# v of unit 1 loaded through GpSimd's queue instead of SP's, with a new order for all engines

## The chip, the cores and the metric

The kernel runs on one core of one Trainium2 chip. The metric is the device time of one execution in microseconds (us), taken over several runs; the median of the runs of the kernel before is 177.78 us (177.57 to 177.90, three runs). The engines are named as in the profile: PE (TensorE matmuls), PEld (its weight loads), DVE (VectorE), ACT (ScalarE), POOL (GpSimd) and SP (SyncE). SPq and POOLq are the queues through which SP and GpSimd issue transfers (DMAs).

## The reference

Two stages. The first is a linear-attention recurrence over 768 steps for each of 4 sequences and 8 heads of width 48; its output, 3072 rows of 384, goes into a feed-forward stage with a squared ReLU.

```python
for t in range(S):
    cur = einsum('bhd,bhe->bhde', u[None] * k[t], v[t])
    y[:, :, t] = einsum('bhd,bhde->bhe', r[t], state + cur)
    state = w[None, :, :, None] * state + einsum('bhd,bhe->bhde', k[t], v[t])
x = y.transpose(0, 2, 1, 3).reshape(B * S, H * D)     # 3072 x 384
out = maximum(x @ w_in, 0) ** 2 @ w_out               # w_in 384 x 2048, w_out 2048 x 384
```

## The kernel before

**Units.** The sequence is cut into 6 chunks of 128 steps; a unit is one chunk of one of the 4 sequences, so there are 24 units, numbered chunk by chunk (units 0 to 3 are the first chunk, and so on). Within a unit the recurrence is done as matrix products: r and k are scaled by powers of the decay (`wpos`, `wneg`), turned, multiplied with each other and masked; the product with v gives the inner part of y, the state of the sequence the rest.

**Steps of a unit.** `load:i:rt`, `load:i:kt`, `load:i:vt` fetch r, k and v of unit i (192 KB each, 1024 pieces of 192 bytes) into `ldr`, `ldk`, `ldv`. `scale:i:0` and `scale:i:1` (DVE, L300) scale r and k into `rkw`; `turn` (PE, L320) and `evict_rk` (ACT, L324) turn them in units 0 to 5, `turn_dma` (a transposing DMA on SP, L309) in the later ones, into `rkT`. `rk` (DVE, L329) multiplies the two; `at` (PE, L337) gives the products of r and k, `mask` (DVE, L349) masks them into `am`. `cast_v` (ACT, L304) makes the bf16 copy `vb` of v. `sums` (PE, L357 and L362) needs `rk`, `vb` and the scaled k, `y_mm` (PE, L400, from the second chunk on also L406) needs `am`, `vb` and the state. `diag_v` and `evict_y` (DVE, L371 and L415) finish y as `yb`; `state_add`, `state_decay`, `state_cast` keep the state. `x_turn` and `evict_x` (PE, ACT) turn `yb` into `xT` in units 0 to 5, `x_dma` (a transposing DMA on SP, L424) in the later ones.

**Feed-forward steps.** `mm1:i:m:s` (PE, L447) multiplies `xT` by a part of w_in: twelve products with m = 1 (units 0 to 7, one unit at a time; s is then the quarter of w_in that it reads), six wider ones with m = 2 (two units at a time, s from 0 to 7). `relu` (ACT, L455) and `square` (ACT, L462, or DVE, L464) make `g`; `mm2:i:q` (PE, L471) multiplies four blocks of `g` by quarter q of w_out; `evict_o` (ACT) and `store` (GpSimd's queue, two on SP) write the result. The last unit goes in two halves (`mm2_half`, L486).

**The order.** No scheduler runs: `SCHEDULE` is a string of some 980 words, and the program issues them one after the other, so each engine and each queue has its instructions in the order of the string. A planner wrote the string once. `name@b` names the PSUM banks that a step takes. `fill` (PE, L245) is a product without use, put where PE is to wait in the plan; there are 68, 52 of them ahead of the first `mm1`. The tile pools put waits on DMAs where a buffer is used again.

**Loads.** r, k and v of units 2 to 5 go through GpSimd's queue, all others through SP's (L278). The four quarters of w_in and the four of w_out also go through GpSimd's queue (`weights`, L288 and L291); the first quarter of w_in is released by a small GpSimd copy that reads k of unit 0, the other quarters (the held-back ones) stand further down in the order. GpSimd also computes the decay columns: `u_columns` (L264, L267) waits for the DVE copy `copy_columns` (L261), `end_columns` (L270, L272) follows later. In the kernel before the first transfers are, in order: on SP k0, r0, r1, k1, v0, v1, k6, k9, k7, r6; on GpSimd's queue r2, quarter 0 of w_in, k2, v2, r3, k3, quarters 1 and 2, v3, r4, quarter 3, r5, quarter 0 of w_out, k4, and so on. Unit 1 is finished after unit 2: its `cast_v` and `sums` come after the first `mm1`.

Of the kernel before, what the change touches and what calls it, by code (L numbers as in the profile page):

```python
# [18 lines left out]
load:1:vt weights:kt.0:0:I fill power:0 3*fill load:2:kt power:1 scale:0:0 load:6:kt fill spread_columns@2 scale:1:0  # L19
load:2:vt fill load:9:kt scale:0:1 2*fill copy_columns turn:0:0@3 load:3:rt fill evict_rk:0:0 turn:0:1@4 u_columns  # L20
fill evict_rk:0:1 fill scale:2:0 turn:1:0@5 load:3:kt fill rk:0 at:0@6,7 scale:1:1 weights:-:1:I fill mask:0:0 fill
turn:1:1@1 cast_v:0 weights:-:2:I mask:0:1 fill evict_rk:1:0 fill load:7:kt fill load:3:vt evict_rk:1:1 y_mm:0@2
2*fill sums:0@3 load:4:rt fill diag_v:0 turn:2:0@4 end_columns rk:1 at:1@6,7 evict_rk:2:0 evict_y:0 2*fill scale:2:1
2*fill x_turn:0@5 mask:1:1 6*fill mask:1:0 3*fill turn:2:1@1 scale:3:0 fill weights:-:3:I evict_rk:2:1 3*fill
scale:3:1 2*fill evict_x:0 fill turn:3:0@4 load:5:rt rk:2 cast_v:2 fill at:2@2,7 load:6:rt fill mask:2:0 fill
weights:-:0:O fill mm1:0:1:0@6 state_add:0 load:4:kt turn:3:1@1 relu:0:1:0 3*fill mask:2:1 fill cast_v:1 mm1:0:1:1@5
weights:-:1:O evict_rk:3:0 sums:1@2 state_cast:0 fill load:4:vt diag_v:1 sums:2@3 y_mm:1@6 relu:0:1:1 y_mm:2@7
evict_y:1 fill mm1:0:1:2@4 evict_rk:3:1 load:5:vt diag_v:2 fill rk:3 x_turn:1@5 at:3@6,1 evict_x:1 evict_y:2
load:5:kt fill relu:0:1:2 fill mask:3:0 3*fill cast_v:3 mm1:1:1:1@5 square:0:1:1:0 square:0:1:0:1 load:8:kt sums:3@7
mask:3:1 x_turn:2@4 mm1:1:1:0@6 evict_x:2 diag_v:3 relu:1:1:1 y_mm:3@1 state_add:1 weights:-:2:O mm1:2:1:2@4  # L30
relu:1:1:0 square:0:1:2:1 evict_y:3 mm1:2:1:1@5 square:1:1:0:1 state_add:3 weights:-:3:O mm1:2:1:0@6 state_add:2
x_turn:3@2 fill evict_x:3 mm1:2:1:3@1 scale:4:0 relu:2:1:2 fill mm1:1:1:3@7 relu:2:1:1 square:2:1:2:1 square:2:1:1:0
mm1:0:1:3@3 relu:2:1:0 mm1:3:1:1@2 square:2:1:0:1 mm1:3:1:3@4 relu:3:1:1 scale:4:1 mm2:1:0@5 square:1:1:1:1
relu:1:1:3 turn:4:0@6 mm2:0:0@2 relu:0:1:3 load:7:rt mm1:1:1:2@7 relu:2:1:3 evict_rk:4:0 fill turn:4:1@3 fill
mm1:3:1:0@1 evict_rk:4:1 cast_v:4 rk:4 mm2:1:1 scale:5:0 relu:1:1:2 at:4@6,0 relu:3:1:0 mm2:2:0@3 mask:4:1
state_cast:2 turn:5:0@7 mask:4:0 sums:4@1 square:1:1:2:1 mm2:0:1 scale:5:1 evict_rk:5:0 diag_v:4 y_mm:4@0 mm2:2:1
evict_y:4 turn:5:1@6 scale:6:1 mm2:0:2 evict_rk:5:1 state_add:4 square:3:1:0:1 x_turn:4@7 mm2:2:2 square:0:1:3:0
evict_x:4 square:3:1:1:1 at:5@0,6 load:6:vt mm2:3:0@1 state_cast:3 mask:5:1 mm1:4:1:0@7 square:1:1:3:0 load:8:rt
state_cast:1 rk:5 mm2:3:1 cast_v:5 mask:5:0 relu:3:1:3 mm2:0:3 square:2:1:3:0 mm1:4:1:3@6 scale:6:0 mm2:2:3
relu:4:1:3 turn_dma:6 relu:4:1:0 sums:5@0 y_mm:5@4 diag_v:5 mm1:4:1:2@6 load:8:vt scale:7:1 evict_y:5 mm1:4:1:1@7  # L40
relu:4:1:2 scale:7:0 square:4:1:0:1 mm2:1:2 state_decay:4 turn_dma:7 square:4:1:3:0 x_turn:5@4 mm2:1:3 evict_x:5
square:3:1:3:0 relu:4:1:1 mm2:4:0@6 load:7:vt evict_o:0 square:4:1:1:0 mm1:5:1:3@4 store:0:POOL load:9:rt scale:8:0
mm2:4:1 relu:5:1:3 scale:8:1 load:10:rt evict_o:1 rk:6 at:6@7,2 square:4:1:2:1 mm1:5:1:1@4 mask:6:1 cast_v:6
turn_dma:8 mm1:5:1:0@5 mask:6:0 relu:5:1:1 state_add:5 mm2:4:2 relu:5:1:0 square:5:1:1:1 mm1:5:1:2@2 sums:6@4
relu:5:1:2 mm2:4:3 diag_v:6 square:5:1:0:1 state_decay:5 y_mm:6@7 cast_v:7 rk:7 at:7@5,0 evict_y:6 square:5:1:2:1
mm2:5:0@2 mask:7:1 x_dma:6 mm1:3:1:2@7 state_add:6 mm2:5:1 relu:3:1:2 load:10:kt mask:7:0 load:9:vt sums:7@0
square:3:1:2:1 scale:9:1 mm2:5:2 evict_o:4 diag_v:7 y_mm:7@4 state_cast:4 store:4:POOL scale:9:0 at:8@7,5 evict_y:7
cast_v:8 turn_dma:9 mm2:3:2 store:1:POOL rk:8 mm1:6:1:0@6 square:5:1:3:0 x_dma:7 scale:10:0 sums:8@4 relu:6:1:0
mm2:5:3 state_add:7 mm1:6:1:1@6 evict_o:5 load:11:kt state_decay:6 square:6:1:0:1 mask:8:1 load:11:rt mm1:6:1:3@0
state_cast:5 scale:10:1 mm2:6:0@2 mask:8:0 state_cast:6 mm2:3:3 diag_v:8 turn_dma:10 relu:6:1:1 y_mm:8@5 relu:6:1:3  # L50
mm1:6:1:2@7 evict_y:8 cast_v:9 square:6:1:1:0 x_dma:8 at:9@6,0 relu:6:1:2 mm1:7:1:1@5 rk:9 square:6:1:2:1
square:6:1:3:0 sums:9@7 load:12:rt evict_o:2 mm2:6:1 mask:9:1 relu:7:1:1 load:10:vt store:2:POOL mask:9:0 mm2:6:2
store:5:POOL state_add:9 mm1:7:1:0@3 y_mm:9@0 diag_v:9 relu:7:1:0 mm1:7:1:3@5 scale:11:1 square:7:1:1:1 evict_y:9
mm1:7:1:2@6 evict_o:3 scale:11:0 square:7:1:0:1 x_dma:9 store:3:POOL mm2:6:3 relu:7:1:3 mm2:7:0@7 relu:7:1:2
square:7:1:3:0 turn_dma:11 at:10@3,0 square:7:1:2:1 state_decay:7 mm2:7:1 rk:10 mask:10:1 load:11:vt mm2:7:2
mask:10:0 load:12:kt cast_v:10 mm2:7:3 state_add:8 state_cast:7 load:13:kt sums:10@1 mm1:8:2:0@5 evict_o:6
state_decay:8 load:12:vt diag_v:10 state_cast:8 y_mm:10@6 mm1:8:2:1@0 evict_y:10 relu:8:2:0 state_decay:9
mm1:8:2:6@3 x_dma:10 relu:8:2:1 rk:11 scale:12:0 state_cast:9 at:11@4,2 mm1:8:2:2@6 mask:11:0 load:13:rt cast_v:11
mm1:8:2:5@5 square:8:2:0:1 mask:11:1 relu:8:2:2 mm1:8:2:3@0 scale:12:1 relu:8:2:6 square:8:2:1:0 turn_dma:12
sums:11@4 square:8:2:2:1 mm1:8:2:4@2 diag_v:11 relu:8:2:3 scale:13:1 mm2:8:0@6 load:14:rt relu:8:2:5 square:8:2:3:0  # L60
y_mm:11@3 square:8:2:6:1 mm2:9:0@0 evict_y:11 relu:8:2:4 scale:13:0 mm2:9:1 x_dma:11 square:8:2:5:1 state_add:11
cast_v:12 mm2:8:1 square:8:2:4:1 turn_dma:13 mm1:8:2:7@5 mm2:8:2 relu:8:2:7 load:14:kt mm2:9:2 square:8:2:7:0
load:13:vt at:12@3,2 rk:12 mm2:8:3 mask:12:1 load:15:kt sums:12@4 mask:12:0 evict_o:8 mm1:10:2:0@5 store:8:POOL
load:15:rt state_decay:11 state_add:10 y_mm:12@2 relu:10:2:0 store:6:POOL mm1:10:2:1@6 square:10:2:0:1 rk:13
load:16:rt mm1:10:2:3@3 diag_v:12 relu:10:2:1 evict_y:12 mm1:10:2:2@5 scale:14:0 x_dma:12 at:13@1,6 relu:10:2:2
square:10:2:1:0 mm1:10:2:4@2 relu:10:2:3 scale:14:1 cast_v:13 mm1:10:2:6@5 square:10:2:3:0 turn_dma:14 mm2:9:3
relu:10:2:6 mask:13:1 relu:10:2:4 sums:13@3 mask:13:0 mm1:10:2:7@5 load:14:vt square:10:2:2:1 scale:15:1
mm1:10:2:5@6 square:10:2:4:1 diag_v:13 evict_o:7 y_mm:13@2 relu:10:2:7 store:7:POOL mm2:10:0@1 evict_y:13
relu:10:2:5 scale:15:0 mm2:11:0@7 square:10:2:6:1 state_add:12 mm2:11:1 square:10:2:5:1 square:10:2:7:0 x_dma:13
mm2:10:1 state_decay:12 mm2:10:2 turn_dma:15 rk:14 at:14@5,2 state_decay:10 mm2:10:3 mask:14:1 state_cast:10  # L70
load:16:kt mm2:11:2 mask:14:0 cast_v:14 load:15:vt evict_o:9 mm1:12:2:0@6 state_add:13 load:17:rt state_cast:12
store:9:POOL y_mm:14@4 load:17:kt scale:16:0 sums:14@2 relu:12:2:0 mm1:12:2:1@5 diag_v:14 state_cast:11 mm1:12:2:2@0
evict_y:14 relu:12:2:1 state_add:14 x_dma:14 at:15@3,6 square:12:2:0:1 mm1:12:2:7@4 rk:15 state_decay:13
mm1:12:2:3@5 relu:12:2:7 scale:16:1 relu:12:2:2 mask:15:0 mm1:12:2:5@2 turn_dma:16 square:12:2:2:1 mask:15:1
mm2:11:3 cast_v:15 square:12:2:1:0 load:16:vt mm1:12:2:6@4 relu:12:2:3 state_decay:14 sums:15@0 square:12:2:3:0
relu:12:2:6 y_mm:15@3 load:18:rt evict_o:10 mm2:12:0@6 diag_v:15 state_cast:14 store:10:POOL state_add:15
mm1:12:2:4@5 relu:12:2:5 evict_y:15 mm2:13:0@4 relu:12:2:4 scale:17:0 x_dma:15 mm2:13:1 square:12:2:5:1 scale:17:1
square:12:2:4:1 at:16@1,0 square:12:2:7:0 mm2:12:1 square:12:2:6:1 load:18:kt mask:16:0 turn_dma:17 state_cast:13
# [38 lines left out]
def kernel(  # L117
# [11 lines left out]
    nc = tc.nc  # L129
# [13 lines left out]
    PAIRED = ()  # L143

    const = ctx.enter_context(tc.tile_pool(name="const", bufs=1))
    room = {'ldr': 3,
            'ldk': 8,
            'ldv': 4,
            'rkw': 4,
# [408 lines left out]
```

## Time and profile before

| what | us |
|---|---|
| median of the runs | 177.78 |
| the profiled execution, its own time | 176.95 |
| its span in the trace | 175.1 |
| PE busy | 167.7 |
| DVE busy | 128.8 |
| ACT busy | 128.1 |
| POOL busy | 33.2 |

The span is what the trace covers; the execution's own time is 1.9 us longer. A busy engine in this table is one with an instruction in flight; matmuls overlap, so the step from one group's start to the next says more than their busy time. Where an engine waits, the view of waits says for how long and for whom; the chain of waits goes back from the last instruction to what released each one. A DMA is listed by its issue, and the view of one tile gives the time from issue to landing, the moment when its last piece has arrived.

### The profile page before, as it was taken

What the parts mean: (1) busy time and instruction counts of PE and PEld (TensorE: products, weight loads), DVE (VectorE), ACT (ScalarE), POOL (GpSimd) and SP (SyncE); (2) the same over time, 40 slices, a digit from 0 to 9 for tenths busy, and PEclk for the clock granted to TensorE, in tenths of its full rate; (3) what the DMA queues carried; (4) which work ended last, traced back from release to release, by engine and by line L of the source; (5) the groups of instructions that cost most, each with busy time, mean ns of one, the idle gap of its engine ahead of it and who ended that gap; (6) DMA issues with size and microseconds to landing.
All of it is one profiled execution on the core that took longest, in us unless ns stands there. A gap on an engine that the chain in (4) does not pass through costs nothing.

```text
span 175.1 us, 4846 instructions
## 1 busy us (share of the span) xinstructions
PE 167.7 (96%) x1946; PEld 132.1 (75%) x1946; DVE 128.8 (74%) x280; ACT 128.1 (73%) x266; POOL 33.2 (19%) x66
## 2 busy tenths in 40 slices
PE   7869999999999999999999999999999999999992
PEld 3547999777787888696786886986886886878870
DVE  4459797199788998997998999689988497550400
ACT  4344798977787797799486989299498595992951
POOL 8998560000010203000201101010110011120010
PEclk9999999999999999999999999999999999999999
DMA  5999999978595999999999998998999987521013
GB/s 109 196 221 191 215 231 249 197 139 160 108 217 106 193 159 215 198 196 155 178 236 170 230 118 188 205 131 190 207 172 170 161 165 201 112 78 35 4 45 135
DMA packets 93848, 28.83 MB, mean 165 GB/s; under 512 B 89681, under 2 KB 91730, under 8 KB 93826
## 3 DMA queue, kind: packets, MB, share of 16 engines
q1 hardware_dynamic: 89472, 18.88, 63.5%
q0 software_dynamic: 4352, 9.64, 22.7%
q8 instruction: 15, 0.25, 0.6%
q14 instruction: 7, 0.06, 0.2%
q10 hardware_dynamic: 2, 0.00, 0.0%
HBM read 20.45 MB, written 4.72 MB: 144 GB/s over the span
## 4 chain that ended last, share of the span: by engine, by line
PE 76%; DMA 9%; ACT 6%; DVE 4%; SPq 2%; issue 1%; DVEq 0%
PE bank L447 31%; PE bank L471 30%; DMA ldv<-in_v_dram 4%; PE bank L337 4%; DMA rkT<-rkw 3%; PE bank L245 2%; PE bank L400 2%; PE bank L362 2%; ACT gr L455 2%; DMA xT<-yb 2%; SPq L278 2%; PE bank L406 2%; PE bank L486 2%; ACT g L462 1%; DVE g L464 1%; ACT osb L478 1%
## 5 line engine op out<-in xcount | busy, mean ns | idle before, releaser
L447 PE MATMUL bank<-xT,w_in_q 128*128 128x128 bf16 (+1 forms) x768 | 72.4, 246 | 0.3 <-DMA xT<-yb 0.3
L455 ACT ACTIVATE gr<-bank 128x512 f32<-128x512 f32 x96 | 53.7, 603 | 20.2 <-PE bank L447 18.9
L471 PE MATMUL bank<-w_out_q,g 128*128 128x384 bf16 x368 | 68.5, 326 | 0.0
L447 PEld LDWEIGHTS <-w_in_q 128*128 128x128 bf16 x768 | 64.1, 114 | 3.6 <-issue 0.5
L471 PEld LDWEIGHTS <-g 128*128 128x128 bf16 x368 | 33.5, 98 | 18.4
L462 ACT ACTIVATE g<-gr 128x512 bf16<-128x512 f32 x60 | 37.0, 641 | 0.4
L505 POOL DMA_DIRECT2D out_dram<-osb x21 | 11.3, 542 | 131.5 <-ACT osb L478 120.3
L349 DVE TENSOR_TENSOR am<-bank,smask 128x512 bf16<-128x512 f32 x48 | 31.5, 683 | 1.9 <-PE bank L337 1.5
L464 DVE TENSOR_TENSOR g<-gr 128x512 bf16<-128x512 f32 x36 | 24.5, 685 | 9.9 <-ACT gr L455 9.7
L371 DVE TENSOR_TENSOR dv<-vb,bank 128x384 f32<-128x384 bf16 x24 | 13.2, 549 | 7.5 <-PE bank L362 4.6
L300 DVE TENSOR_TENSOR rkw<-ldr,wpos 128x384 bf16<-128x384 f32 x24 | 13.2, 551 | 5.2 <-DMA ldr<-in_r_dram 2.6
L415 DVE TENSOR_TENSOR yb<-bank,dv 128x384 bf16<-128x384 f32 x24 | 13.3, 554 | 4.8 <-PE bank L406 4.1
L391 ACT CAST stb<-st 64x192 bf16<-64x192 f32 x40 | 13.9, 349 | 2.4 <-DVE st L385 2.0
L304 ACT CAST vb<-ldv 128x384 bf16<-128x384 f32 x24 | 12.3, 513 | 3.8 <-DMA ldv<-in_v_dram 3.5
L478 ACT COPY osb<-bank 128x384 f32<-128x384 f32 x23 | 11.0, 486 | 5.5 <-PE bank L471 5.4
L245 PE MATMUL bank<-warm 128*128 128x256 bf16 x68 | 13.6, 315 | 1.2 <-DVE warm L193 1.2
L329 DVE TENSOR_TENSOR rk<-rkT 128x512 bf16<-128x512 bf16 x24 | 10.0, 419 | 5.8 <-ACT rkT L324 4.3
L300 DVE TENSOR_TENSOR rkw<-ldk,wneg 128x384 bf16<-128x384 f32 x24 | 13.2, 550 | 0.3 <-DMA ldk<-in_k_dram 0.3
L381 DVE TENSOR_TENSOR st<-bank,st 64x192 f32<-64x192 f32 x32 | 11.2, 351 | 0.2
L324 ACT COPY rkT<-bank 128x512 bf16<-128x512 bf16 x12 | 6.9, 585 | 6.0 <-PE bank L320 5.9
L400 PE MATMUL bank<-vb,am 128*128 128x48 bf16 x192 | 8.6, 183 | 1.4 <-ACT vb L304 1.4
L400 PEld LDWEIGHTS <-am 128*128 128x128 bf16 x192 | 7.8, 96 | 2.6 <-issue 1.4
(61 smaller groups left out, 115.6 us busy)
## 6 DMA issues: line engine op xcount, KB each, us to landing
out_dram<-osb POOLq DMA_DIRECT2D x21, 192.0 KB, 3.3
ldk<-in_k_dram SPq DMA_DIRECT2D x20, 192.0 KB, 4.0
ldr<-in_r_dram SPq DMA_DIRECT2D x20, 192.0 KB, 4.1
ldv<-in_v_dram SPq DMA_DIRECT2D x20, 192.0 KB, 4.0
w_in_q<-in_moe_w_in_dram POOLq DMA_DIRECT2D x4, 384.0 KB, 8.6
w_out_q<-in_moe_w_out_dram POOLq DMA_DIRECT2D x4, 384.0 KB, 11.4
ldr<-in_r_dram POOLq DMA_DIRECT2D x4, 192.0 KB, 8.4
ldk<-in_k_dram POOLq DMA_DIRECT2D x4, 192.0 KB, 8.7
```

Of the source, the lines that this page charges most:

```text
L245: nc.tensor.matmul(out=bank("fill")[:, :WIDE], lhsT=warm[:, :128], rhs=warm, start=True, stop=True)
L300: nc.vector.tensor_tensor(t["rkw"][:, x, :, :, :D], pair(src), pair(wx), ALU.mult)
L349: nc.vector.tensor_tensor(am, t["at"][o], smask.unsqueeze(1).to_broadcast([C, HP, C]), ALU.mult)
L371: nc.vector.tensor_tensor(t["dv"], t["vb"], t["d"].unsqueeze(2).to_broadcast([C, H, D]), ALU.mult)
L391: nc.scalar.copy(stb[b][sl, :, o * D : (o + 1) * D], st32[b][sl])
L400: nc.tensor.matmul(out=y[:, 2 * p + o, :], lhsT=t[f"am{o}"][:, p, :], rhs=t["vb"][:, 2 * p + o, :], start=(o == 0 and p == 0), stop=c == 0 ...
L415: nc.vector.tensor_tensor(t["yb"], t["y"], t["dv"].rearrange("p h d -> p (h d)"), ALU.add)
L447: nc.tensor.matmul(out=t["h", s][:, a], lhsT=turned, rhs=chunks[c]["xT"][:, n, b : b + m, :], start=(n == 0), stop=(n == NK - 1),)
L455: nc.scalar.activation(t["gr", s], t["h", s], AF.Relu)
L462: nc.scalar.activation(g, x, AF.Square)
L464: nc.vector.tensor_tensor(g, x, x, ALU.mult)
L471: nc.tensor.matmul(out=t["o"], lhsT=chunks[units[i][0]]["g"][:, f, units[i][1], :], rhs=w_out_q[f // 4][:, f % 4, :], start=(f == 0), stop ...
```

## The change

v of unit 1 goes through GpSimd's queue. In that queue the first transfers are now r2, quarter 0 of w_in, r3, k2, v1, k3, quarter 1, v2, quarter 2, v3, quarter 3, r4, quarter 0 of w_out, k4, quarter 1 of w_out, r5, v4, and so on; `u_columns` stands between r3 and k2, `end_columns` between v3 and quarter 3. On SP they are k0, r0, r1, k1, v0, k6, r6, r7, k7, v8, r8, k8. The pool `ldr` has four tiles instead of three, `ldv` five instead of four. All engines have a new order: the string is another one throughout. It has as many words and as many fills as the one before, 49 of the fills ahead of the first `mm1`, and every step of the one is in the other. Unit 1's `cast_v` and `sums` now stand ahead of the first `mm1`, and `mm1:0:1:3`, the last part of unit 0, ahead of most of units 1 and 2.

```diff
 SCHEDULE = """
 load:0:kt fill@0 load:0:rt 2*fill load:1:rt 2*fill load:1:kt fill columns 2*fill spread_log@1 load:0:vt load:2:rt
-load:1:vt weights:kt.0:0:I fill power:0 3*fill load:2:kt power:1 scale:0:0 load:6:kt fill spread_columns@2 scale:1:0
-load:2:vt fill load:9:kt scale:0:1 2*fill copy_columns turn:0:0@3 load:3:rt fill evict_rk:0:0 turn:0:1@4 u_columns
-fill evict_rk:0:1 fill scale:2:0 turn:1:0@5 load:3:kt fill rk:0 at:0@6,7 scale:1:1 weights:-:1:I fill mask:0:0 fill
-turn:1:1@1 cast_v:0 weights:-:2:I mask:0:1 fill evict_rk:1:0 fill load:7:kt fill load:3:vt evict_rk:1:1 y_mm:0@2
...
+load:6:kt weights:kt.0:0:I fill power:0 3*fill load:3:rt power:1 scale:0:0 spread_columns@2 load:6:rt scale:0:1
+turn:0:0@3 scale:1:0 fill copy_columns evict_rk:0:0 load:7:rt fill u_columns turn:1:0@4 turn:0:1@5 load:2:kt fill
+evict_rk:0:1 fill scale:2:0 fill evict_rk:1:0 fill load:1:vt rk:0 2*fill scale:1:1 fill turn:2:0@6 load:3:kt 2*fill
+turn:1:1@7 weights:-:1:I at:0@1,2 cast_v:0 load:2:vt evict_rk:2:0 fill mask:0:1 2*fill evict_rk:1:1 sums:0@3
+mask:0:0 weights:-:2:I 2*fill diag_v:0 fill load:3:vt y_mm:0@5 scale:3:0 2*fill scale:2:1 2*fill end_columns fill
+load:7:kt at:1@4,6 rk:1 cast_v:1 fill evict_y:0 2*fill turn:3:0@2 mask:1:0 sums:1@7 fill turn:2:1@1 diag_v:1 fill
+evict_rk:2:1 3*fill mask:1:1 4*fill x_turn:0@5 weights:-:3:I scale:3:1 fill evict_x:0 2*fill at:2@4,1 evict_rk:3:0
+load:4:rt mm1:0:1:0@6 mask:2:0 fill mask:2:1 weights:-:0:O turn:3:1@5 mm1:0:1:1@2 evict_rk:3:1 rk:2 cast_v:2
+load:4:kt fill y_mm:1@4 relu:0:1:0 fill evict_y:1 2*fill y_mm:2@1 relu:0:1:1 weights:-:1:O 2*fill sums:2@5 fill
+diag_v:2 at:3@6,4 load:5:rt x_turn:1@2 evict_y:2 fill evict_x:1 3*fill state_add:1 fill load:4:vt x_turn:2@1
+mm1:1:1:0@2 evict_x:2 mask:3:1 weights:-:2:O cast_v:3 mm1:0:1:2@7 rk:3 relu:1:1:0 state_add:2 fill mm1:2:1:2@1
+square:1:1:0:1 load:8:vt load:5:kt mask:3:0 relu:0:1:2 mm1:1:1:1@4 square:0:1:0:1 square:0:1:1:0 weights:-:3:O
+mm1:0:1:3@2 relu:2:1:2 state_add:0 mm1:2:1:0@5 square:0:1:2:1 scale:4:0 square:2:1:2:1 y_mm:3@7 sums:3@6 relu:1:1:1
...
-    room = {'ldr': 3,
+    room = {'ldr': 4,
             'ldk': 8,
-            'ldv': 4,
+            'ldv': 5,
...
-        (nc.gpsimd if i in (2, 3, 4, 5) else nc.sync).dma_start(
+        (nc.gpsimd if i in (2, 3, 4, 5) or name + str(i) in ('vt1',) else nc.sync).dma_start(
```

Near the end, the steps of the last four units stood and now stand so:

```diff
-relu:20:2:7 sums:23@2 square:20:2:1:0 mm1:20:2:6@3 relu:20:2:2 diag_v:23 y_mm:23@7 evict_o:19 square:20:2:7:0
-mm1:20:2:4@1 square:20:2:2:1 store:19:POOL evict_y:23 mm2:20:0@6 relu:20:2:6 store:17:POOL x_dma:23 relu:20:2:4
-mm2:20:1 square:20:2:6:1 mm2:21:0@5 square:20:2:4:1 mm2:21:1 mm2:20:2 mm1:22:2:3@4 mm1:22:2:7@2 mm1:22:2:0@0
+mask:23:1 relu:20:2:5 mm2:19:3 mask:23:0 relu:20:2:2 sums:23@3 mm1:20:2:6@7 diag_v:23 square:20:2:2:1 y_mm:23@1
+square:20:2:5:1 mm2:21:0@4 evict_y:23 square:20:2:4:1 square:20:2:7:0 mm2:20:0@6 x_dma:23 relu:20:2:6 evict_o:19
+mm2:20:1 mm2:20:2 mm2:21:1 mm1:22:2:3@2 mm1:22:2:7@5 mm1:22:2:6@3 relu:22:2:7 relu:22:2:3 mm1:22:2:0@1
```

## The prediction

> **What bounds the kernel now.** I read the page's first rows, then TensorE's waits, the chain of waits, the issues and landings of the early loads, and the end.
>
> ```profile
> PE 167.7 (96%) x1946; PEld 132.1 (75%) x1946; DVE 128.8 (74%) x280; ACT 128.1 (73%) x266; POOL 33.2 (19%) x66
> ...
> DMA  5999999978595999999999998998999987521013
> ...
> PE bank L400 <- ACT vb L304: 1.4, 1, 1.4
> PE bank L258 <- DMA wu<-in_w_dram: 0.5, 1, 0.5
> PE bank L447 <- DMA xT<-yb: 0.3, 1, 0.3
> ...
> 4.06 7.81 DMA ldv<-in_v_dram
> 11.89 0.51 ACT vb L304
> ...
> 155.71 3.23 DMA xT<-yb
> 158.98 3.44 PE bank L447 x30
> ```
>
> TensorE is busy for 96% of the span, and in the timeline its groups follow each other at a fixed rate from 15 us on: 0.67 us for an `mm1` of 12 products, 0.65 for one of 6 wide products or an `mm2` of 4, 0.33 for `at`, 0.22 for `turn`, 0.20 for `y_mm` of the first chunk, 0.26 for `sums`, 0.17 for `x_turn`, 0.11 for a `fill`. Only one gap over 0.25 us is left after 15 us: the last `xT`, at 158.5. So the time is the start (to the first `mm1` at 18.06), plus fixed work, plus a tail. In the start the chain is v of unit 0 (issued 4.06, landed 11.87), its cast, and what hangs on it; the DMA row is full until slice 33 of 40.
>
> ```profile
> L278 SPq DMA_DIRECT2D ldv<-in_v_dram x2: 706/1116/1525, 4.1 to 4.8; - x2
> DMA to landing us min/median/max: 7.8/10.6/13.5
> ...
> L278 POOL DMA_DIRECT2D ldr<-in_r_dram x1: 912/912/912, 7.2 to 7.2; - x1
> DMA to landing us min/median/max: 7.7/7.7/7.7
> ...
> L278 POOL DMA_DIRECT2D ldr<-in_r_dram x1: 957/957/957, 3.6 to 3.6; - x1
> DMA to landing us min/median/max: 5.0/5.0/5.0
> ...
> 15.86 0.76 POOL L288 DMA_DIRECT2D w_in_q<-in_moe_w_in_dram  x1
> ```
>
> These are the views of single tiles in short windows. v of units 0 and 1 go through SP and take 7.8 and 13.5 us: v1, issued at 4.81, lands at 18.3. Loads of the same size through GpSimd take 5.0 (r2), 7.2 (k2), 7.5 (v2), 7.7 (r3) and 7.0 us (k3), the held-back quarters 8.1, 10.0 and 9.1.
>
> **v1 on the other queue.** The schedule of before uses v1 late (cast at 19.43), after unit 2; the new one uses it before the first `mm1`. GpSimd's new order is r2, quarter 0, r3, [columns], k2, v1, k3, quarter 1, v2, quarter 2, v3, [end columns], quarter 3, r4. Issue times by the durations of before: r3 5.45 to 6.36; the columns wait for DVE's copy (7.09 + 0.16) and take 1.03 (8.12 to 9.15 in before), so k2 at 8.3, then v1 9.2, k3 10.1, quarter 1 at 11.0, v2 11.8, quarter 2 at 12.7, v3 13.5, end columns 2.44, quarter 3 at 16.8. No trace shows v1 there. By place it is the fifth transfer of this queue, of the same sizes as the five of before (four loads, one quarter), whose fifth landed at 7.22 + 7.7 = 14.9. By issue it is 9.2 plus 5.0 to 7.7: 14.2 to 16.9. I take 14.9, since the DMA row is full and the row at the same place is the nearest.
>
> A rule speaks against this. The Trainium skill, "DMA: Bandwidth & Descriptors", section "Issuing engines are not separate DMA queues", says that all issuers share the same 16 engines and that another issuer saves only issue time; by it v1 would land at 18.3 whoever issues it. The rows above (13.5 us on SP, 7.0 to 7.7 on GpSimd in the same microseconds) are against it. The same page, section "Anatomy of one DMA — SWDGE (gpsimd) path", gives some 2.0 us plus bytes at 436 GB/s, an estimate of 2.5 us for 192 KB; no load here came under 5.0, and with 2.5 v1 would be no limit at all.
>
> **The start, step by step.** Up to the columns nothing TensorE needs moves. From there, new order: `turn` 0:0, two fills, 1:0, 0:1, seven fills, 2:0, two, 1:1 (its `scale` waits on DVE for `rk:0`: 10.4), `at:0` at 10.6, three fills, 11.3. `sums:0` waits for v0, whose queue ahead of it is unchanged: 11.87, cast 0.51, 12.45. Three fills, `y_mm:0`, five fills, `at:1` at 13.8, three fills, `turn` 3:0 to 14.7. `sums:1` waits for v1: 14.9 + 0.51 + 0.07 = 15.5, so 0.8 us of new wait here and 1.2 at v0; before has, start to start, 1.5 at v0 (12.45 less the last fill's 10.92) and 0.5 at `x_turn:0` (14.82 less 14.33). On DVE `scale:2:1` waits for k2 (fourth in the queue: 6.34 + 7.5 = 13.8) with `rk:1`, `evict_y:0` and `mask:1:0` behind it; 13.8 + 0.5 + 0.5 = 14.8 is before 15.5, so v1 ends last. After that 0.26 (`sums`) + 0.11 + 0.22 (`turn` 2:1) + 0.88 (eight fills) + 0.17 (`x_turn`) + 0.33 + 0.33 (`at:2`) = 2.30: first `mm1` at 17.85 (15.5 + 2.3 and 0.05 for `evict_x:0`). Before: 18.06, so -0.21. Fills are 68 in both, 49 ahead of it instead of 52, thus three more behind (+0.33); `sums:1` is done already (-0.26). Start: **-0.14**. By 14.2 `rk:1` takes over (14.85): -0.8; by 16.9: +1.9.
>
> **The held-back quarters.** With the units in order, `mm1:0:1:3`, the first user of quarter 3, comes 7.11 us after the first `mm1` (six `mm1` 4.02, fourteen fills 1.54, `turn`, two `y_mm`, `sums`, `at`, two `x_turn` 1.55): 24.96. In before its first user was `mm1:2:1:3` at 27.45. It landed at 15.86 + 9.1 = 24.96 there, as eleventh of the queue after seven loads and three quarters; it is eleventh after the same now, but is issued 0.9 later: 24.96 to 25.9. I take 25.3: **+0.35**. Quarter 1 (18.1 to 19.1, wanted at 18.85) and v2 behind it (19.2 to 20.2, wanted at 19.5) are the same lateness seen sooner and do not add. This also caps a gain: however soon v1 lands, `mm1:0:1:3` can't run before 24.96.
>
> **What costs nothing.** The new tiles (`ldr` 4, `ldv` 5) let r6 and r7 go to SP right behind k6, in the place of v1, k9 and k7; SP is blocked in its issues from 8 to 35 us in before, and its loads for units 6 to 8 are wanted after 42; its slack of some 2 us hides it. Without it `turn_dma:6` and all behind it on SP would be late. GpSimd's DMAs are as many, plus one; its later stores are off the chain.
>
> **The rest.** All engines have a new order; TensorE's work is the same to the product. In the order around each transposing DMA I summed TensorE's work between issue and use: least 3.7 us for `rkT` (4.2 before) and 3.25 from `y_mm:23` to its `mm1` (3.9 before), against landings of 3.2 to 5.9 and 2.3 to 5.4. A wait that the order hides on paper can show; between 0 and twice the one that before has, 0.48 + 0.3, I take **+0.3**. At the end `y_mm:23` is no longer followed by squares on DVE ahead of `evict_y:23`: 0.2 + 0.56 + 0.03, then 2.28 (the `xT` at 151.18) to 3.23 (the last one) and 0.04, less 3.25 of cover: a wait of 0 to 0.8 instead of 0.48, so -0.48 to +0.3; I take **-0.1**.
>
> Sum: -0.14 + 0.35 + 0.3 - 0.1 = +0.41. The profiled execution took 176.95 (span 175.1 and 1.9 around it), so 177.36 there; the runs' median is 177.78, so **178.2**.
>
> **Rivals.**
> - *The start costs nothing and the end pays* (faster). The DMA engines bound the start and carry the same bytes ahead of quarter 3; it lands at 24.96 again, start -0.14 and no quarter wait. The wait for the last `xT` then decides: at 2.3 instead of 3.23 it is gone. -0.14 - 0.48 = -0.62: 177.15. It turns at an `xT` landing of 2.8 us. For it: no store is issued near it any more (two at 155.29 in before). Against: a reordered middle without one new wait.
> - *v1 and k2 come late* (slower). Their descriptors are ready only some time after the issue, which GpSimd's columns now delay: k3 took 7.0 us with as little ahead of it. v1 at 16.2, +1.3 on the start; quarter 3 is then in time, so +1.15 and the 0.2 of the other terms: 179.1.
> - *No change.* v1's wait takes the place of v0's, and the terms cancel: 177.8.
> - *The issuer doesn't matter*: v1 still lands at 18.3; first `mm1` at 18.3 + 0.6 + 2.35 = 21.2, +3.2: 181.
>
> **Chances.** Forecast 0.45 (own range 177.7 to 178.8), end pays 0.28, v1 late 0.15, no change 0.09, issuer 0.03. Within 0.2% is 0.36 us, about what a measurement of this kernel can tell. Faster: 0.28 + 0.02 of the forecast's own range + 0.02 of no change = 0.32; same 0.11 + 0.07 = 0.18; slower 0.32 + 0.15 + 0.03 = 0.50. The range goes from the end's full gain with a little of the start's (176.8) to v1 at its late bound (179.5).
>
> **What would show it.** Right: v1's load through GpSimd takes about 5.7 us from issue; TensorE waits some 0.8 us in front of L357 or L362 around 15 us for the cast of v1; first `mm1` near 17.9; a short wait for `w_in_q` around 25. Wrong: v1 landing after 16 or first `mm1` after 19 (the late rival), before 17.3 (queue drained); a wait over 0.5 us between 40 and 150, which no term here foresees; the gap in front of the 30 products at 159 gone, or doubled.

## The result

The changed kernel is slower by a little: 179.31 us (median of 12 runs, 177.64 to 182.9) against 177.76 for the kernel before on the same chip (12 runs). The ratio is 1.0065, with a 95% interval of 1.0037 to 1.0092, so some 1.15 us (0.66 to 1.64). The ratio leaves out slow runs, those more than 1.5% above the fastest of their kernel (three of the changed kernel's, two of the kernel before's), while the medians are of all runs. The profiled execution took 179.4, with a span of 177.6 against 175.1.

Page rows of the changed kernel: busy time, TensorE's granted clock in tenths, and the share of the DMA engines.

```profile
PE 169.7 (96%) x1946; PEld 133.2 (75%) x1946; DVE 129.5 (73%) x280; ACT 129.2 (73%) x266; POOL 33.4 (19%) x67
...
PEclk9998799999999999999999999999999999999999
DMA  5999999991597799999999999999899995431015
```

PE has the same 1946 instructions, and 2.0 us more busy time. The clock row, full in every slice before, has a dip at 13 to 22 us. The waits of PE and the chain of waits (start, length, what) of the same execution:

```profile
PE bank L357 <- DVE rk L329: 1.2, 1, 1.2
PE bank L447 <- DMA xT<-yb: 0.5, 2, 0.2
...
PE bank L362 <- ACT vb L304: 0.4, 1, 0.4
...
7.85 0.82 POOL ldk L278
8.67 7.07 DMA ldv<-in_v_dram
15.76 0.52 ACT vb L304
...
158.38 3.25 PE bank L471 x20
161.63 5.24 PE bank L447 x48
```

The long wait for the cast of v0 (1.4) is gone; v0 landed at 10.34, 1.5 us sooner than in the profile of before. That is spread rather than the change: in e7, e9 and e11, which have the order before, it landed at 11.44, 10.28 and 9.20. In its place PE waits for `rk:1`, which stands on DVE behind `scale:2:1` and so behind k2 (landed 14.68), and then for v1 (15.73). At the end the 48 products follow the 20 without a gap: the wait for the last `xT` is gone. The page's two waits for an `xT` are new ones, at 75.8 (unit 9) and 100.8 (unit 13).

GpSimd's timeline in the changed kernel (start, length, line, operation) shows what stands ahead of k2 and v1:

```profile
5.45 0.92 POOL L278 DMA_DIRECT2D ldr<-in_r_dram  x1
7.14 0.20 POOL L264 TENSOR_TENSOR cols<-cols 128x4 f32<-128x4 f32 x1 [0.77 <-DVE cols L261]
7.41 0.43 POOL L267 CAST uwb<-cols 64x4 bf16<-64x4 f32 x2
7.77 0.91 POOL L278 DMA_DIRECT2D ldk<-in_k_dram  x1
8.67 0.89 POOL L278 DMA_DIRECT2D ldv<-in_v_dram  x1
...
10.41 0.76 POOL L288 DMA_DIRECT2D w_in_q<-in_moe_w_in_dram  x1
```

From 6.37 to 7.77 GpSimd issues nothing: it waits for the DVE copy, then computes the columns. The order before has such a hole too, from 8.13 to 9.15, but behind k2, v2 and r3; the new one is longer by 0.4 us and stands ahead of k2 and v1. It shows in what the queue moves. Summed from the packets in the trace, half a microsecond at a time, GpSimd's queue falls from 196 GB/s (10.5 to 11 us) to 56 and 33 (11 to 12 us); in the profile of before its low is at 13 to 14 us (97 and 64). From 11 to 12 us SP's queue moves 162 and 145 GB/s instead, so the engines stay busy: a full DMA row doesn't tell that one of the queues has run short.

The view by windows (PE busy, PEld, DVE, ACT, POOL, granted clock, DMA share, GB/s) shows what PE did next:

```profile
14.00:15.00 1.00, 0.49 (x7) 0.30 (x4) 0.29 (x1) 0.00 (x0) 0.70 (x4) 1.00 1.12 181
15.00:16.00 1.00, 0.26 (x4) 0.19 (x5) 1.00 (x4) 0.24 (x1) 0.82 (x4) 1.00 1.05 160
16.00:18.00 2.00, 1.68 (x15) 1.34 (x15) 1.91 (x5) 0.86 (x2) 2.00 (x3) 0.70 1.22 204
18.00:20.00 2.00, 2.00 (x18) 1.30 (x16) 0.38 (x1) 0.90 (x2) 1.08 (x2) 0.50 1.18 228
20.00:22.00 2.00, 2.00 (x37) 1.80 (x32) 1.62 (x3) 0.66 (x3) 1.46 (x2) 0.95 1.17 235
```

0.70, 0.50 and 0.95 mean half clock for 1.2 + 2.0 + 0.2 = 3.4 us, from 16.8 to 20.2, some 1.7 us of work. The first `mm1` starts at 20.18 (18.06 before). That accounts for 2.5 of the 2.6 us between the two spans: +2.12 at the start; from the first `mm1` to the last group of products 153.07 for 152.70, so +0.37, which is two waits of 0.40 and 0.41 start to start, three fills more (+0.32) and `sums:1` already done (-0.26), less the 0.48 at the end. The half clock belongs to some runs only: four of the twelve had a mean clock of 0.988 to 0.990 (179.4, 180.33, 180.65, 182.9), the other eight 0.996 or more, with 178.57 on average. These eight are still 0.97 us above the ten lowest of the twelve runs of the kernel before (177.60 on average), so most of the loss is there at full clock too. Of the 74 runs of the kernel before beside the experiments one was under 0.993.

### The profile page after: what moved, and what is told of

It is laid out like the page before. It is cut to its first block, busy times and chain, and to the rows that moved or that the text cites. A ratio compares the mean times of both kernels' runs of the same rounds, so it can differ in the third digit from the quotient of the medians.

```text
span 177.6 us, 4850 instructions
## 1 busy us (share of the span) xinstructions
PE 169.7 (96%) x1946; PEld 133.2 (75%) x1946; DVE 129.5 (73%) x280; ACT 129.2 (73%) x266; POOL 33.4 (19%) x67
## 4 chain that ended last, share of the span: by engine, by line
PE 78%; DMA 10%; ACT 5%; DVE 3%; issue 1%; POOL 1%; ACTq 0%; DVEq 0%
PE bank L447 33%; PE bank L471 28%; DMA xT<-yb 6%; DMA ldv<-in_v_dram 4%; PE bank L337 3%; PE bank L245 2%; PE bank L400 2%; PE bank L362 2%; ACT gr L455 2%; PE bank L406 2%; PE bank L486 1%; DVE yb L415 1%; PE bank L249 1%; PE bank L357 1%; DVE rkw L300 1%
## 5 line engine op out<-in xcount | busy, mean ns | idle before, releaser
L471 PE MATMUL bank<-w_out_q,g 128*128 128x384 bf16 x368 | 67.7, 326 | 0.0
L462 ACT ACTIVATE g<-gr 128x512 bf16<-128x512 f32 x60 | 36.3, 632 | 0.6
L464 DVE TENSOR_TENSOR g<-gr 128x512 bf16<-128x512 f32 x36 | 24.3, 685 | 10.8 <-ACT gr L455 10.5
L245 PE MATMUL bank<-warm 128*128 128x256 bf16 x68 | 14.7, 341 | 1.2 <-DVE warm L193 1.2
L245 PEld LDWEIGHTS <-warm 128*128 128x128 bf16 x68 | 7.2, 119 | 4.0 <-DVE warm L193 1.2
L337 PE MATMUL bank<-rkT 64*128 64x128 bf16 x192 | 9.7, 222 | 0.0
```

The source lines that it names most:

```text
L245: nc.tensor.matmul(out=bank("fill")[:, :WIDE], lhsT=warm[:, :128], rhs=warm, start=True, stop=True)
L337: nc.tensor.matmul(out=t["at"][o][:, p, :], lhsT=t["rkT"][sl, 1, p, :], rhs=t["rkT"][sl, 0, p, :], start=True, stop=True,)
L462: nc.scalar.activation(g, x, AF.Square)
L464: nc.vector.tensor_tensor(g, x, x, ALU.mult)
L471: nc.tensor.matmul(out=t["o"], lhsT=chunks[units[i][0]]["g"][:, f, units[i][1], :], rhs=w_out_q[f // 4][:, f % 4, :], start=(f == 0), stop ...
```

## The experiments

"New order" is the changed kernel's; the diffs cut the string to the words concerned. The ratios are to the kernel before on the same chip. The medians are of six or twelve runs on several chips, on which the kernel before had 177.15 to 177.76, so rows compare by their ratios.

| kernel | median us | ratio, 95% interval |
|---|---|---|
| changed kernel | 179.31 | 1.0065 (1.0037 to 1.0092) |
| e1 new order, columns behind v1 | 177.76 | 1.0026 (1.0005 to 1.0047) |
| e2 new order, 11 more fills | 179.81 | 1.0130 (1.0088 to 1.0173) |
| s1 new start, old rest | 179.92 | 1.0174 (1.0128 to 1.0220) |
| s2 old start, new rest | 180.61 | 1.0159 (1.0110 to 1.0209) |
| e3 new order, v1 on SyncE | 199.85 | 1.1256 (1.1220 to 1.1293) |
| e5 e1 and two middle edits | 177.89 | 1.0039 (1.0016 to 1.0063) |
| e6 the two middle edits alone | 179.97 | 1.0106 (1.0058 to 1.0154) |
| e7 old order, v1 on GpSimd | 179.33 | 1.0090 (1.0057 to 1.0124) |
| e8 e5, r12 moved back | 178.46 | 1.0065 (1.0040 to 1.0089) |
| e9 old order, columns ahead of k2 | 178.36 | 1.0067 (1.0045 to 1.0089) |
| e10 e1 without 19 late fills | 177.09 | 0.9998 (0.9975 to 1.0020) |
| e11 old order without 16 late fills | 177.41 | 1.0027 (1.0001 to 1.0053) |

### e1: the columns behind v1

```diff
 copy_columns evict_rk:0:0 load:7:rt fill
-u_columns
 turn:1:0@4 turn:0:1@5 load:2:kt fill
 evict_rk:0:1 fill scale:2:0 fill evict_rk:1:0 fill load:1:vt
+u_columns
```

> The changed kernel with one step moved: u_columns stands behind v of unit 1 in GpSimd's queue instead of ahead of k of unit 2. Theory (the columns let GpSimd's queue run dry at 11 us, so k2 lands at 14.7 and v1 at 15.7, TensorE idles some 2 us at sums:1 and then runs 3.4 us at half clock): k2 lands at 13.8 or sooner, v1 at 14.9 or sooner, the wait at sums:1 shrinks by 0.8 us or more, the half clock around 17 us is gone, and the first mm1 comes at 17.9 or sooner instead of 20.2; the time is 1 to 2.5 us below the changed kernel's, 176.5 to 178. Rival (the loss is in the new order behind 40 us): the start gains as said, but the time stays at 178.5 or more. Rival (the DMA engines bound it anyway): k2 and v1 land as late as before, no change.

GpSimd's timeline of e1:

```profile
5.45 0.93 POOL L278 DMA_DIRECT2D ldr<-in_r_dram  x1
6.35 0.91 POOL L278 DMA_DIRECT2D ldk<-in_k_dram  x1
7.22 0.91 POOL L278 DMA_DIRECT2D ldv<-in_v_dram  x1
8.12 0.24 POOL L264 TENSOR_TENSOR cols<-cols 128x4 f32<-128x4 f32 x1
```

k2 and v1 land at 13.34 and 14.70, 7.0 and 7.5 us after their issue, and quarter 1 at 17.91 in place of 19.74. So k2 lands 1.34 sooner for an issue 1.42 sooner: the gap in the issues comes back as a gap in the landings. The transfers behind it, from v1 to quarter 3, land 0.6 to 1.8 us sooner. The time falls from 1.0065 to 1.0026. The two intervals still overlap a little; two more comparisons bear on it, e5 against e6, and e9, which makes the gap in the order before. The profiled execution itself tells nothing of the start: v0, on SP, landed at 14.43 there, PE waited 2.4 us for it and got the half clock; the other eleven runs had 0.996 or more.

### e2: fills in the wait

```diff
 turn:3:0@2
+11*fill
 mask:1:0 sums:1@7
```

> The changed kernel with eleven more fills between turn:3:0 and sums:1, where TensorE was idle for 1.2 us in the profile (1.2 us of products without use). Theory of the clock (an idle TensorE around 15 us is answered with half clock from 16.8 to 20.2, at a cost of 1.7 us): waits and landings stay, the granted clock stays at 1.00 through 16 to 22 us in the profile, fewer of the runs have a granted clock under 0.995, first mm1 at 18.5 to 18.9, time 0.5 to 1.7 us below the changed kernel's. Rival (the waits alone cost the time and the half clock comes from something else): half clock stays, time the same or 0.2 us more.

The clock stayed at 1.00 in the profile and at 0.996 or more in all six runs, and the first `mm1` came at 18.87 with v1 at 15.99. The time rose all the same, to 1.013, so the expected gain did not come. That the fills keep the clock is not shown by this: eight of the changed kernel's twelve runs kept it without them, and so did five of e6's six. The fills do not bring k2 and v1, and with them the kernel is no faster than the changed one. The profiled execution, at 178.43, was the lowest of the six; what held up the others (179.48 to 181.48) no trace shows.

### s1 and s2: two halves of the two orders

In these two the PSUM bank of `mm2:7` is taken again, around the seam, ahead of its reader `evict_o:7`, so that results are others; PE's work is the same.

```diff
-new order
+s1: new order up to mm1:8:2:0, then the order before
+s2: order before up to sums:10 (v1 on GpSimd behind r2), then the new order
```

> The changed kernel's order up to the first mm1 of unit 8, the order of the kernel before from there on, with the changed kernel's tile rooms. Theory (the loss is in the first 20 us): as slow as the changed kernel, 178.5 to 179.5. Rival (the loss is in the new order of the later units): as the kernel before, 177.4 to 178.1.

> The order of the kernel before up to sums:10 (v of unit 1 in its old place in the order, but through GpSimd's queue, right behind r2 and ahead of quarter 0 of w_in), the changed kernel's order from there on and its tile rooms. Theory (the loss is in the first 20 us of the new order): near the kernel before, 177.2 to 178.4; v1 ahead of quarter 0 puts all of GpSimd's transfers back by one load, 1.1 us, so up to 1 us more where a quarter is late. Rival (loss in the later units): 178.5 to 179.5 with waits behind 80 us.

Both totals are spoilt by the joint. In s2 v1 ahead of quarter 0 pushes the quarters back (quarter 0 lands at 14.14, quarter 1 at 21.54, against 11.25 and 18.12 before); s1 has new waits at its seam. Only their waits are read: s1, with the old rest, keeps the last `xT` wait (0.48 at 161.5), s2, with the new rest, has the waits for `xT` of units 9 and 13 (0.84 and 1.00) and none at the end. So these three go with the rest of the order and not with the moved load. The two new ones are not firm, though: in e2's profile, with the same rest, only unit 13 waits (0.15), and e11, which keeps the order before but for its late fills, waits for unit 9 (0.33).

### e3: the load back on SyncE, in the new order

```diff
-        (nc.gpsimd if i in (2, 3, 4, 5) or name + str(i) in ('vt1',) else nc.sync).dma_start(
+        (nc.gpsimd if i in (2, 3, 4, 5) else nc.sync).dma_start(
```

> The changed kernel, whose order stays word for word, with v of unit 1 issued by SyncE again, at its place in the list (behind r of unit 7). In the changed kernel v of unit 1 lands at 15.7 us and its cast to bf16 runs at once; before, by SyncE, it landed at 24 us behind the same neighbours. Theory (the new order only stands because GpSimd brings v of unit 1 early): it lands at 17 us or later, sums:1 waits 1 us or more beyond what it waits in the changed kernel, and the run is 0.8 to 3 us above the changed kernel's 179.3, ratio 1.013 to 1.025 against before. Rival (the issuer of one load does not matter, both queues feed the same 16 DMA engines and the bytes are the same): it lands within 1 us of 15.7 and the time stays within 0.4 us of the changed kernel's.

Clock row, waits and chain of e3:

```profile
PEclk9999555599999999999999999999999999999998
...
PE bank L362 <- ACT vb L304: 21.4, 1, 21.4
...
9.44 26.98 DMA ldv<-in_v_dram
```

v1 lands at 36.42, PE stands for 21.4 us, and the kernel loses 22.6 against the kernel before. The rival (the issuer does not matter) is out by far, and so is the size in my own expectation. (In the kernel before v1 landed at 18.29, not at 24, and with other neighbours.) The place differs as well as the issuer: in the new order k6, r6 and r7 stand ahead of v1 on SP. They land at 13.07, 20.07 and 30.78: 393 KB (r6, r7) in 17.7 us, 22 GB/s. In the same stretch GpSimd's queue moved 3.54 MB, 200 GB/s. The Trainium skill, "DMA: Bandwidth & Descriptors", section "Queues, rings and completion order", says that each DMA engine goes round the queues that have work for it, packet by packet. The trace agrees: counted from its packets, GpSimd's queue finished 2012 and SP's 2032 between 13.07 and 30.78. So the two queues had a packet each in turn, as far as the counts can show, and the rates stand as the sizes do: 192 KB are 1024 packets of 192 bytes on SP's queue and 48 of 3840 or 4224 bytes on GpSimd's.

### e7: the load moved, the order before

```diff
-load:1:vt weights:kt.0:0:I
+weights:kt.0:0:I
...
-load:3:rt
+load:3:rt load:1:vt
...
-            'ldv': 4,
+            'ldv': 5,
```

It has the changed `dma_start` line too.

> The kernel before, in its own order, with only the load moved: v of unit 1 issued by GpSimd behind r of unit 2, the first quarter, r of unit 3 and k of unit 2, and one more buffer for v (5). The sums of unit 1 stand where they stood, behind mm1:0:1:0. Theory (the moved load costs and brings nothing by itself, what counts is the order planned around it): v of unit 1 lands at 14 to 17 us with its cast still where it was, the quarters of w_in land up to 1 us later, and the time is 0.998 to 1.003 of before. Rival (the load itself is the harm: 0.9 us more of GpSimd's issue and 192 KB ahead of the quarters): first mm1 or the quarters late by 0.5 us or more, the time 1.004 to 1.010.

PE's timeline of e7, where `mm1` first reads quarters 1 and 2:

```profile
20.53 0.86 PE L447 MATMUL bank<-xT,w_in_q 128*128 128x128 bf16 x12 [1.40 <-DMA w_in_q<-in_moe_w_in_dram]
...
23.09 0.86 PE L447 MATMUL bank<-xT,w_in_q 128*128 128x128 bf16 x12 [0.54 <-DMA w_in_q<-in_moe_w_in_dram]
```

v1, issued at 8.11, lands at 16.22. In the kernel before SP issued it at 4.81 and it landed at 18.29: with the order otherwise the same, GpSimd's issue comes 3.3 us later and the data 2.1 us sooner. But v1 is not wanted before 19, and quarter 1, one load further back, lands at 20.48 (18.12 before) and PE waits 1.9 us in all. The rival holds, in size too: by itself the moved load costs 0.9%. The new order puts v2 behind quarter 1 in exchange; with the columns out of the way (e1) quarter 1 lands at 17.91, no later than in the kernel before.

### e9: the gap alone, in the order before

```diff
-load:2:kt power:1 scale:0:0 load:6:kt fill spread_columns@2 scale:1:0 load:2:vt
+power:1 scale:0:0 load:6:kt fill spread_columns@2 scale:1:0
...
-evict_rk:0:0 turn:0:1@4 u_columns
+evict_rk:0:0 turn:0:1@4 u_columns load:2:kt load:2:vt
```

> The kernel before with one thing of the change: r of unit 3 and the two column instructions go ahead of k and v of unit 2 on GpSimd (r2, quarter 0, r3, columns, k2, v2, k3, quarter 1), all loads by the engines that had them. Theory (a load lands no sooner than some 6.6 to 7 us after its issue, so the 1.4 us in which GpSimd issues nothing return as a hole in its queue): k of unit 2 is issued at 7.8 in place of 5.45 and lands at 14.4 to 14.9 in place of 12.7, quarter 1 lands at 19 to 20 in place of 18.1, and PE waits 0.3 to 1.2 us for one or the other: 1.002 to 1.007 of before. Rival (the queue has work for those 1.4 us anyway and catches up): k of unit 2 lands by 13.9, quarter 1 by 18.4, the time within 0.002 of before.

GpSimd's and PE's timelines of e9:

```profile
6.29 0.90 POOL L278 DMA_DIRECT2D ldr<-in_r_dram  x1 [0.81 <-DVE rkw L300]
7.32 0.20 POOL L264 TENSOR_TENSOR cols<-cols 128x4 f32<-128x4 f32 x1
7.59 0.43 POOL L267 CAST uwb<-cols 64x4 bf16<-64x4 f32 x2
7.95 0.91 POOL L278 DMA_DIRECT2D ldk<-in_k_dram  x1
```

```profile
16.84 0.40 PE L320 MATMUL bank<-identb,rkw 128*128 128x128 bf16 x4 [0.44 <-DVE rkw L300]
19.67 0.86 PE L447 MATMUL bank<-xT,w_in_q 128*128 128x128 bf16 x12 [0.23 <-DMA w_in_q<-in_moe_w_in_dram]
22.22 0.86 PE L447 MATMUL bank<-xT,w_in_q 128*128 128x128 bf16 x12 [0.52 <-DMA w_in_q<-in_moe_w_in_dram]
```

Here r3 itself waits for one of three `ldr` buffers, so the gap is in two pieces, but k2 is issued at 7.95, as in the changed kernel (7.77). It lands at 14.50 (6.6 later) and holds DVE up for 0.49 us, so that a scaled product two steps on (16.24) is late for PE; quarter 1 lands at 19.63. The three waits of PE are 1.2 us in all. Every size came as expected, and the rival (the queue catches up) is out. The ratio, 1.0067, is as large as the changed kernel's loss, without v1 and without the new order's other parts. Not all of it is the columns' place: r3 now stands ahead of k2 and v2 and waits 0.8 us for its buffer, and part of k2's lateness may be r3's place. Ahead of quarter 1, however, stand the same six transfers as before, and it lands 1.51 us later; that part is the holes in the issues. It is also where the time goes: the first `mm1` comes at 17.95, no later than before (18.06, with v0 landing 1.6 us later there), and what follows takes 1.04 us longer.

### e5, e6 and e8: the two waits in the middle

```diff
 y_mm:9@7
+evict_y:9
 state_add:8 relu:7:1:0 mm1:7:1:3@6 square:7:1:0:1 scale:11:1 mm1:7:1:2@4 evict_o:3
-evict_y:9
...
 mm2:11:2 state_cast:10 load:17:kt
+mm2:11:3
 mm1:12:2:0@6
...
-mm2:11:3
```

e6 is the new order with this, e5 has the columns of e1 beside it, and e8 has in addition:

```diff
-load:12:rt
...
 load:11:vt
+load:12:rt
```

> The changed kernel with u_columns behind load:1:vt (as in the run before with that edit, 1.0026 of before) and with the two new waits in the middle covered: evict_y:9 directly behind y_mm:9 on VectorE (1.2 us earlier), and mm2:11:3 (0.66 us of PE) ahead of mm1:12:2:0. Theory (the time is the start plus the waits that PE cannot cover, and those two are worth 0.57 and 0.46 us in that run): both waits fall under 0.1 us, the time falls by 0.6 to 1.0 us against the kernel with the columns alone, to 0.997 to 0.999 of before. Rival (what is won in the middle comes back later, at the last xT or at the last bank): the waits go but another of 0.4 us or more appears behind them, and the time stays at 1.001 to 1.004.

> The changed kernel with the two middle edits alone: evict_y:9 directly behind y_mm:9 on VectorE, mm2:11:3 ahead of mm1:12:2:0. Theory: PE's waits for xT of units 9 and 13 (0.40 and 0.41 us in the changed kernel's profile) fall under 0.1 us, and the time by 0.6 to 0.9 us, to 1.001 to 1.003 of before, with the start as late as in the changed kernel. Rival (given back later): the time stays at 1.005 to 1.008.

> As e5_columns_and_middle, with the load of r of unit 12 moved on SyncE's queue from ahead of the transposition into xT of unit 9 to behind v of unit 11. In e5 evict_y:9 ran earlier, yet xT of unit 9 landed only at 74.4, 4.7 us after its issue, behind r of unit 12 (71.7) and v of unit 10 (72.9), and PE still waited 0.55 us. Theory (the wait is set by the 393 KB that stand ahead of it in the same queue): xT of unit 9 lands 0.8 to 1.2 us earlier against its issue (3.5 to 3.9 us), the wait falls under 0.1 us, and the time falls by 0.3 to 0.6 us against e5, to 1.000 to 1.002 of before. Rival (all queues are full there, so that it lands 4.5 us or more after its issue whatever stands ahead): the wait stays over 0.4 us and the time at 1.003 to 1.005.

PE's timeline of e5, and then two lines of e8's:

```profile
74.41 1.47 PE L447 MATMUL bank<-xT,w_in_q 128*128 128x256 bf16 x12 [0.39 <-DMA xT<-yb]
```

```profile
74.08 1.50 PE L447 MATMUL bank<-xT,w_in_q 128*128 128x256 bf16 x12 [0.40 <-DMA xT<-yb]
...
85.63 0.40 PE L337 MATMUL bank<-rkT 64*128 64x128 bf16 x8 [0.49 <-DMA rkT<-rkw]
```

The wait for unit 13 goes in all three. The one for unit 9 stays: its transfer takes longer, 4.7 us in e5, 5.0 in e6 and 4.7 in e8, where r12 no longer stands ahead of it, against 3.5 in the changed kernel. The edit also did less than expected: counted from the first `mm1`, the transfer is issued 0.4 us sooner in e5, 0.3 in e6 and not at all in e8, instead of 1.2, since DVE now waits for `y_mm:9` ahead of `evict_y:9`. In e8 the load that was put back makes `rkT` of unit 12 late (0.49), and the `xT` of unit 11 is waited for too (0.37). None of the three gained: e5 stands at 1.0039 (e1 1.0026), e6 at 1.0106 (changed kernel 1.0065), e8 at 1.0065. So one of the two waits could be taken away, and no time came of it; what the other is worth, and what holds `xT` of unit 9 back, is not settled. Between e5 and e6, which differ in the columns' place alone, stand 0.0067, with intervals that touch.

In e6, at full clock, the start can be read without the dip: first `mm1` at 18.30, and then

```profile
19.96 0.86 PE L447 MATMUL bank<-xT,w_in_q 128*128 128x128 bf16 x12 [0.46 <-DMA w_in_q<-in_moe_w_in_dram]
```

Quarter 1 (19.91) is the limit behind v1. In the profile of the changed kernel it landed at 19.74 too, but there the first `mm1` started at 20.18, behind it.

### e10 and e11: the late fills

```diff
-load:4:kt fill y_mm:1@4 relu:0:1:0 fill evict_y:1 2*fill y_mm:2@1
+load:4:kt y_mm:1@4 relu:0:1:0 evict_y:1 y_mm:2@1
...
```

> The changed kernel with u_columns behind load:1:vt and without the 19 fills that stand behind mm1:0:1:0 (before has 16 there; each is one matmul of 128x256, 0.107 us). Theory (a fill stands where PE would wait anyway): the time stays within 0.4 us of the kernel with the columns alone, 1.000 to 1.005 of before, with PE waiting instead, mostly between 18 and 28 us. Rival (they cost their own time): 2.0 us less, 0.989 to 0.993.

> The kernel before without the 16 fills that stand behind mm1:0:1:0 in its list (1.7 us of PE at 0.107 us each). With the 19 late fills gone, the changed order with the columns behind v of unit 1 fell from 1.0026 to 0.9998 of before, some 0.5 us. Theory (those fills are longer than the waits that they cover, in both orders alike): 0.996 to 0.999 of before, and so ahead of both kernels. Rival (they only cost something in the new order, whose first quarter of an hour of matmuls waits less): 0.999 to 1.003, with PE waits between 18 and 28 us that add up to the fills.

(By the "first quarter of an hour" the text means the first matmuls behind `mm1:0:1:0`.) PE's waits in e10:

```profile
PE bank L431 <- DVE yb L415: 0.6, 1, 0.6
...
PE bank L400 <- ACT vb L304: 0.6, 1, 0.6
```

In e10 the time is that of before (0.9998), 0.0028 under e1: of the 2.0 us of fills some 0.5 would have been paid, and the rest comes back as waits. The intervals of e1 and e10 overlap, so the 0.5 us is likely and not shown. From the first `mm1` on the profiled execution takes 152.60 us (e1 153.32, before 152.70). In the old order the same cut gains nothing (1.0027). No version here is shown to be ahead of the kernel before.

## Why the prediction was right, and where it was not

The direction, the range and the place (the start) were right. The forecast's sum of +0.41 was short of some 1.15, and the mechanism that came was the rival *v1 and k2 come late*, at 179.1, which had a chance of 0.15. Two of the prediction's own signs of being wrong came: the first `mm1` after 19 in the profiled execution, and the gap at the last `xT` gone.

- **Start, -0.14: this step failed.** The issues were, if anything, earlier than assumed (k2 7.77 for 8.3, v1 8.67 for 9.2). The landing of v1 was taken by place in the queue ("the fifth landed at 14.9"), and that of k2 likewise (13.8; it landed at 14.68). But the issue counts too: through GpSimd the 192 KB loads issued between 5.4 and 9.6 land 6.9 to 7.7 us later in both profiles, and in e3, e6 and e9 none of them took less than 6.5. Place is not without effect: in s2, with v1 ahead of them, the loads issued from 6.7 to 10.6 take 8.4 to 8.9. So a hole of 1.4 us in the issues was not caught up. The DMA row, the ground for going by place, was as full as forecast, but it was SP's packets that filled the hole. 8.67 + 7.07 gives 15.73, inside the bounds (14.2 to 16.9), 0.8 above the value taken. The wait began with k2 and not with v1: `rk:1`, put at 14.8, was done at 15.6 (1.17 us of wait), and v1 then ended last as forecast (0.41). The 17.85 for the first `mm1` is what the order gives without the gap: 17.95, 17.24 and 17.71 in e5, e8 and e10. With it, at full clock, it was 18.30 (e6) and 18.47 (s1); in the order before with v0 as early as there it was 17.86 (e11). The half clock, 1.7 us more in the profiled run, was not foreseen.
- **Quarters, +0.35.** Quarter 3 landed at 25.65, within its bounds, but nothing waited for it, neither there nor at full clock in e5 and e6, where it landed at 25.31 and 25.81. Quarter 1 was said to be "the same lateness seen sooner" at 18.1 to 19.1; it landed at 19.74, and cost 0.46 in e6.
- **What costs nothing.** Held: in none of the profiles of the new order does PE wait for a load of units 6 to 8.
- **The rest, +0.3.** Two new waits, 0.40 and 0.41, together just over the upper bound of 0.78. But taking one of them away gained nothing, so their worth as a cost is not shown.
- **End, -0.1.** It was -0.48, the best case: the wait for the last `xT` is gone in the changed kernel. That half of the faster rival came true and was outweighed.
- **The rule of one set of engines.** By the Trainium skill, "DMA: Bandwidth & Descriptors", section "Issuing engines are not separate DMA queues", another issuer saves only issue time, and v1 would land at 18.3 with either. 16.22 on GpSimd in the same order (e7), 15.73 in the new order, and 36.42 on SP in the new order (e3) are against it.

Where the 1.15 us come from: e1 takes the gap out of the new order, which is worth 0.0039, or 0.69 us, and leaves 0.0026, or 0.46. e5 against e6 and e9 put the gap higher, at 0.0067, or 1.2 us, e9 with the other place of r3 in it. So the gap is the larger part, and its size is known to some half a microsecond. What is left agrees in size with the longer rest (+0.37 in the profile); which part of that costs it is open; the late fills (e10) are likely a part.

## What to carry to other kernels

A transfer is planned by the time of its issue as well as by its place in the queue: an instruction that makes the issuing engine wait ahead of it, here two small column operations behind a copy, leaves a hole in the queue 4 to 5 us later, and what stands behind it comes late (0.6 to 1.8 us between e1 and the changed kernel). This one hole makes the larger part of the loss. Loads that are needed at once belong ahead of such work. A load moved forward on a full queue is paid for by whatever is then behind it, unless another one is moved back (e7 against e1), and of two queues with unlike packets the one with small pieces got little while the other had work (22 against 200 GB/s in e3).

## What the runs showed of the hardware

In the changed kernel's profile the granted clock fell to half for 3.4 us after PE had been busy for 0.49 and 0.26 us in two successive microseconds. In the profile of before PE was busy for 0.08 and 0.55 us from 11 to 13, and the clock stayed at 1.00. The Trainium skill, "TensorE: Matmul & The Clock Gate", Part 1, gives half rate after an idle window of some 3.4 us, and says that the window runs freely. The dip is as long as that window (3.4 us). The idle before it does not reach a window: about 1.25 us in those two microseconds. What decides between the two profiles no run here shows. In e3, with 21.4 us of idle, the row shows half clock for four slices, some 20 us, as the rule has it.

The landing of v0 on SP, with the same four loads ahead of it on that queue, was at 9.1 to 14.4 us in the profiles. This spread can move the start of a single execution by more than the change does: in e1, where v0 landed last, the profiled execution took 180.53 against a median of 177.76.
